# New hand-written orders for TensorE, ScalarE and VectorE in the first part of a fused attention and SwiGLU kernel

## The chip, the core and the metric

The kernel runs on one core of a Trainium2 chip. The metric is the device time of one execution in microseconds (us). In the profile PE is TensorE's matmuls, PEld its weight loads, DVE is VectorE, ACT is ScalarE, POOL is GpSimd and SP is SyncE. POOL and SP issue the transfers; POOL also does some masks, SP nothing else.

## The reference

Attention with 4 sink keys and a window of 128 keys, then a root-mean-square norm and a SwiGLU feed-forward layer (FFN):

```python
# q, k, v: (B, H, S, D) = (4, 8, 768, 64); n_sink = 4, window = 128
scores = q @ k.T / sqrt(D)
rel = pos[:, None] - pos[None, :]
keep = (pos[None, :] < n_sink) | ((rel >= 0) & (rel < window))
a = softmax(where(keep, scores, -1e9))
x = (a @ v).transpose(0, 2, 1, 3).reshape(3072, 512)
xn = x / sqrt(mean(x * x, -1) + 1e-6) * rms_g
g = xn @ w_gate                    # 512 x 1536
silu = g / (1 + exp(-g))
out = (silu * (xn @ w_val)) @ w_out   # w_out: 1536 x 512
```

Inputs and output are float32.

## The kernel before

**Tiling.** The 3072 tokens are 24 blocks g of 128 tokens, six per batch b. Four blocks make one of six FFN groups G of 512 tokens. A block is worked off in these steps; in the orders and below each has a short name:

- q, k and v of block g are loaded with a cast to bfloat16 (`load_bf16`, L353; `load_v`, L357) by POOL. The tile of v, `V16[b]`, holds the six blocks of a batch, with a 65th column per head that is 1.0, so that the product with v also gives the sum of the softmax. That column is written once per batch by a memset on DVE (L278, "vone:b"); the loads into this tile wait for it. The first load into each tile, in POOL's order, is v:0, v:8 (it stands ahead of v:6 and v:7), v:12 and v:18.
- q and k are transposed. Blocks 0 to 7: by PE (`pe_t`, L445) and a copy out of PSUM on DVE or ACT (`copy_t`, L452, "qT:g", "kT:g"). From block 8 on: by DMA transposes in SP's queue (`dma_t`, L459).
- Scores on PE (`scores` L485, `scores_last` L501, `tri_scores` L563, "s:g"). S:g needs k of block g and q of blocks g and g + 1. Scores of the sink keys are "ss" (L742).
- Exponentials on ACT ("x:g"), the mask on DVE (L520, L547, L584) or, from block 16 on, on POOL (L526, L597) ("e:g").
- The product with v on PE (`av`, L616, L621, L641), and the division by the sum on DVE (`normal`, L660, L661, "n:g").
- The square on ACT (`square`, L669, "ms:g"), and the norm on DVE (`rms`, L676 to L693, "xr:g").
- A transpose of the normalised block: by PE and a copy (L708, L714) up to block 7, by DMA in SP's queue (`dma_x`, L720) after that ("xt:g").

The FFN of a group runs over pieces (G, ft, column): gate matmuls (g, L975) and value matmuls (u, L975, out of `wv`), tanh on ACT (L982), `silu` (L988, "p1") and `hidden` (L998, "h", tile hT) on DVE, then the projections ("po", L1008), the copy to SBUF on ACT (L1016) and the store on SP (L1020). Group 0 is cut into pieces of 128 tokens and four column blocks of the weights (16 matmuls of 128 columns), groups 1 and 2 into pieces of 256 tokens and two column blocks (8 matmuls of 256 columns), the others into pieces of 512 tokens.

**The order.** No scheduler decides anything at build time. A class `Plan` numbers the operations as they are described (1077 of them). `ORDER` lists the numbers for each engine, `TURNS` says which engine's next operation is emitted at each step, and `BANKS` gives the PSUM bank of each tile of matmul results. `Plan.run` replays the three and asserts that each operation's needs have been given before. An engine works its list off in order. Each operation waits for what it reads and for the buffers that it writes; an operation that waits holds all that stand behind it on its engine, and a load that waits holds POOL's later loads and masks.

**The queues.** POOL's loads go in the order of `LOADS`, in which v:8 stands 33rd, behind the weights, and ahead of q:8, v:5, k:6, k:7, k:8, v:6, v:7 and q:9. The loads rotate through eight semaphores, so that a load is issued only when the load eight places ahead of it has landed. SP's queue begins with a few small loads; its transposes come in the order qT:8, qT:9, kT:8, kT:9, qT:10, qT:11, kT:10, kT:11, qT:12, qT:13, kT:12, kT:13, qT:14, then mixed with stores and xt.

In the description of the operations a few names only steer or check the plan: `LOAD_LEAD` and `T_LEAD` let a load or a transpose come only after a certain block's scores, `GATE_FROM` and `gate_of` tie the scores of a block to the progress of the FFN. They are requirements that `Plan.run` asserts, and issue no instruction.

Of the kernel before, what the change touches and what calls it, by code (L numbers as in the profile page):

```python
# [12 lines left out]
BF16 = mybir.dt.bfloat16  # L13
I32 = mybir.dt.int32

P = 128
# [18 lines left out]
class Plan:  # L35
# [33 lines left out]

ORDER = {  # L70
    "PE": """
# [18 lines left out]
""",  # L90
    "ACT": """
24 20 22 199 177 175 178 176 182 180 181 183 168 188 222 204-206 211 207 212 209 191 210
217 226 228 227 229 195 598 220 236 603 613 618 608 243 633 628 260 623 245 247 246 248
638 278 262 255 264-267 197 280 282 284 653 273 320 648 643 295 297 659 290 322 299 301
300 302 276 324 325 293 326 327 309 664 678 669 683 674 333 312 693 340 316 341 688 342
343 698 355-357 336 358 703 370 371 708 372 318 373 349 385 364 387 718 713 723 739 379
399 401 400 402 728 418 419 733 420 393 421 409 763 758 778 768 754 773 744 749 427 433
414 783 434-436 448 449 793 450 798 451 442 808 788 819 803 463-466 813 457 824 480 475
482 494 496 497 495 513 488 514 515 504 834 838 516 848 843 853 829 863 868 858 878 873
525 883 531-533 893 509 888 534 899 923 549-551 928 552 938 543 567-569 918 570 585 587  # L100
933 943 948 561 953 579 958 909 904 968 593 963 914 973 1008 1003 994 998 1013 1028 1023
989 1038 1018 1033 984 1053 1048 1043 979 1069 1059 1064 1072 1073
""",
    "DVE": """
# [24 lines left out]
""",  # L129
}  # L130
TURNS = """
ASDDSDGDPDPSPDPPPPPGPPPGPDPGPPDDPGAGPPPPADGPPPPGPPSPDPSADPGSDPSPGAAAPAGPAPPDAPPGPPAPDPAP
PPPADPGPDAGPPDPPDGAPPGPAPPAGDPAPAPDGADAPDGPAPPPADPAGPDAPADAGPPPPAPADGAPADGPPPPPAPPDPGPPD
DPAGPDPAGPDPGAPDDGPDGPDADGDPDGPADADPGAADPGPGDPADGAPDPGADAPGADADPGDPAPPDAPPDADAPGDPPADAGP
AAGPAPDAPPDPADPDAPGDAPDDGDPAPGDPPGSAAPGADAPGDPDGPPPDAGDAPGDADPPGADPAGDSAPPAGASPADPADSADP
PPGADAPGPSADDPGASAPGDPGSAPPGDPSADGAPDASDAPPDADPAGPPSAAADPAADPADPDAPAGADPGADPPDAPPADDPDGS
PDAPASAGDPPAPAGDSPADAPADDPPAGSADPPDASDPAGPADPSDDPGAPDDPADAPDGSDPDGPAGAPADSAPPADSDPPDGPDS
PDAGASPAAPDASGDPADSPDSDPGSPPPDDPSDGPDADPAPADPSDPSPDPSPDDAPDPDAPADPADAPDADAPDPDPASAPDASAP
DSADPADPDPASAPASADPAPPDASDPDAPSDASPADPDADPDPDPDAPASAPPDASADPAGPDGPGDPDGAPDPDPDPDAPAAGPSA
DGPAASGPADSPAGDPPGDDPGPPDGPDAAGPPDAGADPAGPAAGDPADAGPGPDSPGDPDASGPDGAADSPDAPDSDPPDSPDAPDS  # L140
ADPDSAPPDSDPSDAPDASPADDPDPDPADAPAAPDASADPADSPGSDGPDGSPGPGPAPAPADPAPDADPADAPDAGAPDGPGPAAP
AAPPADGDPPDGPDGDGPPAAPDSPGDPGAGPDAPPDPDPDPDAADPADPDDPAPAADPSDPDPDDPAAPPSPDDPAAPDPPSPPDPA
PSDSDSPASDPDPPPAAPDDPDPDPPAAPSDPDPAPDDPDPPPPAAPDADPSDPAAPDPDPAAPDDPDPDAPADPDPDPDPPDPAAPD
SPSDPPPPPAAPSASSPAADS
"""
BANKS = """
0123456701234567012345645645635654353513714370432704614654154761061305147237235720165760
7615743764051726351402376152376015237653746573746574631547613547647136210735462047136524
7012473650241762350741602735410721356421305406354063420675134632745013274350174362507431
6542371607152374153275461237104573604156324175032407615342047562310462317460170414217326  # L150
5047314243270172316412040572153042573045
"""


# [1 line left out]
def kernel(  # L156
# [15 lines left out]
    B, H, S, D = q.shape  # L172
# [29 lines left out]
    X_DMA_FROM = 8  # L202
    QK_DMA_FROM = 8
    LD = 16
    GATE_FROM = 8
    LOAD_LEAD = 10
    LEAD_FROM = 10
    WARM = 56
    GATE_LEAD = 14
    T_LEAD = 4  # L210
    SPLIT = (0,1)
    CHUNKS = (4,2,2)
    GB_PRIO = 2000
# [3 lines left out]
    HOST_FROM = 8  # L217

    const = ctx.enter_context(tc.tile_pool(name="const", bufs=1))
    ld = ctx.enter_context(tc.tile_pool(name="ld", bufs=LD))  # L220
    vld = ctx.enter_context(tc.tile_pool(name="vld", bufs=B))
    qkt = ctx.enter_context(tc.tile_pool(name="qkt", bufs=2))
    sink = ctx.enter_context(tc.tile_pool(name="sink", bufs=2))
# [108 lines left out]
        )  # L332

    for i in range(NS):
        sp(430, 2600, lambda i=i: load_sink(i), ["vsink1", "grow"], [("vsink", i)], -70 + i)

# [8 lines left out]
        eng.dma_start(out=T["st", name, g], in_=block_of(src, g))  # L345

    def cast(name, g, copy):
        T[name, g] = ld.tile([P, H, D], BF16, name=name)
        copy(out=T[name, g], in_=T.pop(("st", name, g)))

    def load_bf16(name, src, g):
        T[name, g] = ld.tile([P, H, D], BF16, name=name)
        nc.gpsimd.dma_start(out=T[name, g], in_=block_of(src, g))  # L353

    def load_v(g):
# [27 lines left out]

    def sw_block(g, what="qkv"):
        for n in what:
            needs = [("s", g - LOAD_LEAD)] if g >= LEAD_FROM else []
            if n == "v":
                sw_load(lambda g=g: load_v(g), [("v", g)], 860,
                        needs=needs + [("vone", g // NT)])
            else:  # L390
                src = q if n == "q" else k
                needs += [(n + "T", g - LD)] if g >= LD else []
                sw_load(lambda n=n, src=src, g=g: load_bf16(n, src, g), [(n, g)], 860,
                        needs=needs)
# [477 lines left out]
    for g in range(NB):  # L872
# [9 lines left out]
        for n in "qk":  # L882
            if g < QK_DMA_FROM:
                pe(225, lambda n=n, g=g: pe_t(n, g), [(n, g), "ident"] + old, [(n + "p", g)],
                   pa, takes=[(n, g)])
                ways = {"DVE": (345, lambda n=n, g=g: copy_t(n, g, nc.vector.tensor_copy)),
                        "ACT": (470, lambda n=n, g=g: copy_t(n, g, nc.scalar.copy))}
                either(ways, [(n + "p", g), "table"], [(n + "T", g)], early, drops=[(n, g)])
            else:
                sp(1290, 1200, lambda n=n, g=g: dma_t(n, g),  # L890
                   [(n, g)] + old + [("s", g - T_LEAD)], [(n + "T", g)], g,
                   ring="TR", work=1000)

        if t + 1 == NT:
# [57 lines left out]

        if t == 0:
            dve(600, lambda b=b: sink_k(b),
                [("kT", g), ("s", g + 1)] + ([("ss", b - 2, i) for i in ((2, 4) if b - 2 < 2 else (2,))]
                               if b >= 2 else []), [("ksk", b)], 0.1 * g)
            dve(640, lambda b=b: sink_v(b), [("vsink", i) for i in range(NS)] + ["headm"]
                + ([("av", NT * (b - 2) + NT - 1, u) for u in range(2)] if b >= 2 else []),
# [182 lines left out]
```

## Time and profile before

| | |
|---|---|
| median of 3 runs | 241.89 us (241.77 to 242.81) |
| profiled execution, span | 241.9 us |
| granted TensorE clock | 1.000 |
| DMA, software queue (POOL's loads) | 13.90 MB in 81760 packets, 79.3% of 16 engines' span |
| DMA, hardware queue q1 | 12.95 MB in 31810 packets, 29.8% |
| 0 to 22 us: PE busy, DVE busy | 18.75, 14.52 us |
| 22 to 72 us | 47.05, 44.34 us of 50 |
| 114 to 190 us | 75.15, 64.00 us of 76 |
| 190 to 241.9 us | 48.72, 24.69 us of 51.9 |

The span is the time from the first to the last instruction of one profiled execution. Busy time is the time in which the engine executed instructions; an engine with little idle time can't take more work without making the kernel longer. "L563" is a line of the code printed above. In a timeline each line has a start, a duration, the engine, the line and the operation with its tiles and shape; brackets hold the idle time of the engine just before it and what ended that. The "DMA to landing" of a load is the time from its issue to its completion.

### The profile page before, as it was taken

The numbers are of one execution on the slowest core, as the hardware profiler recorded it, in microseconds if no ns is written. First come the engines' busy times: TensorE is split into PE (matmuls) and PEld (weight loads), VectorE is DVE, ScalarE is ACT, GpSimd is POOL, SyncE is SP. The second block draws the span as 40 slices with busy tenths as digits, with TensorE's granted clock in tenths as the row PEclk, the third lists the DMA queues.
The fourth block names the chain that finished last, engine by engine and source line by source line (L and its number), as shares of the span: only waits on it lengthen the run. The fifth ranks groups of instructions, "written<-read, shape, count | busy, mean of one in ns | idle before, by whom it ended". The sixth has DMA issues, their size and how long they took to land.

```text
span 241.9 us, 5897 instructions
## 1 busy us (share of the span) xinstructions
PE 231.3 (96%) x2329; PEld 147.6 (61%) x2354; DVE 187.4 (77%) x478; ACT 122.8 (51%) x267; POOL 89.2 (37%) x116
## 2 busy tenths in 40 slices
PE   7889999999879999999999999999999999999995
PEld 5568986876668776777876644445554444444443
DVE  3599989989979999999898989994569946537520
ACT  4776368667766574337654464454543321233112
POOL 8985894597526554000004982022540000000000
PEclk9999999999999999999999999999999999999999
DMA  9999999999999999999601999527010114101024
GB/s 128 143 183 195 182 178 194 162 143 139 137 151 152 138 143 154 132 233 156 126 2 24 119 150 123 131 70 128 3 23 0 32 36 173 43 0 47 0 87 173
DMA packets 113741, 27.42 MB, mean 113 GB/s; under 512 B 103857, under 2 KB 110769, under 8 KB 113714
## 3 DMA queue, kind: packets, MB, share of 16 engines
q0 software_dynamic: 81760, 13.90, 79.3%
q1 hardware_dynamic: 31810, 12.95, 29.8%
q8 instruction: 18, 0.29, 0.5%
q10 hardware_dynamic: 144, 0.20, 0.2%
q14 instruction: 9, 0.07, 0.1%
HBM read 28.35 MB, written 6.29 MB: 143 GB/s over the span
## 4 chain that ended last, share of the span: by engine, by line
PE 67%; DMA 20%; POOL 6%; issue 2%; DVE 2%; SPq 2%; POOLq 0%
PE v L975 20%; PE o L1008 20%; PE g L975 18%; DMA wo<-in_moe_w_out_dram 5%; DMA qkT<-q 4%; DMA wv<-in_moe_w_val_dram 4%; DMA wg<-in_moe_w_gate_dram 3%; DMA q<-in_q_dram 3%; POOL v L357 2%; SPq L459 2%; PE s L563 2%; PE av L621 2%; POOL k L353 1%; PE av L616 1%; PE o_last L1028 1%
## 5 line engine op out<-in xcount | busy, mean ns | idle before, releaser
L975 PE MATMUL v<-xnt,wv 128*128 128x128 bf16 (+2 forms) x527 | 72.2, 282 | 0.4 <-DMA wv<-in_moe_w_val_dram 0.2
L975 PE MATMUL g<-xnt,wg 128*128 128x128 bf16 (+2 forms) x521 | 71.3, 281 | 0.4
L1008 PE MATMUL o<-wo,hT 128*128 128x512 bf16 x259 | 65.3, 379 | 1.1 <-issue 0.5
L982 ACT ACTIVATE th<-g 128x512 bf16<-128x512 f32 x72 | 41.7, 599 | 48.4 <-PE g L975 48.2
L988 DVE SCALAR_TENSOR_TENSOR p<-th,g 128x512 bf16<-128x512 bf16 x72 | 48.1, 682 | 18.9 <-ACT th L982 18.7
L975 PEld LDWEIGHTS <-wv 128*128 128x128 bf16 x528 | 43.3, 98 | 21.3 <-DMA wv<-in_moe_w_val_dram 0.6
L998 DVE TENSOR_TENSOR hT<-p,v 128x512 bf16<-128x512 bf16 x72 | 48.1, 682 | 9.3 <-PE v L975 7.8
L975 PEld LDWEIGHTS <-wg 128*128 128x128 bf16 x528 | 42.8, 98 | 19.3 <-issue 1.0
L1008 PEld LDWEIGHTS <-hT 128*128 128x128 bf16 x276 | 25.4, 98 | 26.5 <-issue 0.2
L597 POOL TENSOR_SCALAR_AFFINE_SELECT e<-e 128x512 bf16<-128x512 bf16 x20 | 12.7, 656 | 54.4 <-ACT e L572 53.0
L572 ACT ACTIVATE e<-s 128x384 bf16<-128x384 f32 x52 | 23.1, 495 | 12.5 <-PE s L563 12.5
L1016 ACT ACTIVATE osb<-o 128x512 f32<-128x512 f32 x23 | 13.4, 597 | 21.8 <-PE o L1008 18.0
L357 POOL DMA_DIRECT2D v<-in_v_dram x24 | 21.3, 888 | 8.5 <-DMA q<-in_q_dram 3.8
L353 POOL DMA_DIRECT2D q<-in_q_dram x23 | 20.4, 891 | 9.9 <-DMA k<-in_k_dram 6.7
L353 POOL DMA_DIRECT2D k<-in_k_dram x23 | 20.4, 889 | 9.1 <-DMA v<-in_v_dram 4.5
L669 ACT ACTIVATE sq<-x 128x512 bf16<-128x512 bf16 x24 | 15.1, 631 | 14.8 <-DVE x L661 14.5
L661 DVE TENSOR_TENSOR x<-av,rden 128x256 bf16<-128x256 f32 x48 | 20.4, 424 | 1.7
L693 DVE SCALAR_TENSOR_TENSOR xr<-x,r,gb 128x512 bf16<-128x512 bf16 x24 | 18.7, 778 | 0.8
L621 PE MATMUL av<-v,e 128*128 128x65 bf16 x192 | 16.4, 193 | 0.3 <-DMA v<-in_v_dram 0.3
L536 ACT ACTIVATE e<-s 128x512 bf16<-128x512 f32 (+1 forms) x36 | 15.1, 519 | 1.6 <-PE s L485 1.5
L616 PE MATMUL av<-v,e 128*128 128x65 bf16 x160 | 14.8, 193 | 0.0
L621 PEld LDWEIGHTS <-e 128*128 128x128 bf16 x192 | 12.7, 97 | 2.8 <-DVE e L547 0.4
(78 smaller groups left out, 192.6 us busy)
## 6 DMA issues: line engine op xcount, KB each, us to landing
out_dram<-osb SPq DMA_DIRECT2D x23, 256.0 KB, 2.2
v<-in_v_dram POOLq DMA_DIRECT2D x24, 128.0 KB, 8.9
q<-in_q_dram POOLq DMA_DIRECT2D x23, 128.0 KB, 8.1
k<-in_k_dram POOLq DMA_DIRECT2D x23, 128.0 KB, 9.6
wo<-in_moe_w_out_dram POOLq DMA_DIRECT2D x2, 768.0 KB, 11.3
wg<-in_moe_w_gate_dram POOLq DMA_DIRECT2D x5, 256.0 KB, 8.0
wv<-in_moe_w_val_dram POOLq DMA_DIRECT2D x5, 256.0 KB, 8.9
stage<-in_k_dram SPq DMA_DIRECT2D x1, 256.0 KB, 3.0
```

The lines of the kernel that those rows point to most:

```text
L353: nc.gpsimd.dma_start(out=T[name, g], in_=block_of(src, g))
L357: nc.gpsimd.dma_start(out=V16[b][:, t, :, 0:D], in_=block_of(v, g))
L572: nc.scalar.activation(out=e_tile(g)[:, x:x + 2, 0:TW], in_=BANK.pop(("s", g, u, hi))[:, 0:2 * TW].rearrange("p (j c) -> p j c", c=TW), fu ...
L616: nc.tensor.matmul(out=dest, lhsT=T["e", g - 1][:, x, P:2 * P], rhs=V16[b][:, t - 1, h, :], start=(t == 1), stop=False, skip_group_check=True,
L621: nc.tensor.matmul(out=dest, lhsT=T["e", g][:, x, 0:P], rhs=V16[b][:, t, h, :], start=(t == 0), stop=True, skip_group_check=True,)
L661: nc.vector.tensor_tensor(out=T["x16", g][:, 4 * u:4 * u + 4, :], in0=pvv[:, :, 0:D], in1=rden.unsqueeze(2).to_broadcast((P, 4, D)), op=AL ...
L693: nc.vector.scalar_tensor_tensor(out=T["xr", g], in0=T.pop(("x16", g)).rearrange("p h d -> p (h d)"), scalar=r[:, 3:4], in1=gb, op0=ALU.mu ...
L975: nc.tensor.matmul(out=ps[:, i * n:(i + 1) * n], lhsT=w_sb[:, kt, ft * P:(ft + 1) * P], rhs=T["xnt", G][:, kt, cols], start=(kt == 0), sto ...
L982: nc.scalar.activation(out=T["th", key], in_=BANK[("g", key)], func=ACT.Tanh, scale=0.5,)
L988: nc.vector.scalar_tensor_tensor(out=T["p1", key], in0=T.pop(("th", key)), scalar=1.0, in1=BANK.pop(("g", key)), op0=ALU.add, op1=ALU.mult,)
L998: nc.vector.tensor_tensor(out=T[hk][:, i:i + n, cols], in0=T.pop(("p1", key)).rearrange("p (n c) -> p n c", n=n), in1=BANK.pop(("v", key)) ...
L1008: nc.tensor.matmul(out=BANK[("o", G, tb)], lhsT=T["h", G, ft // 4][:, ft % 4, tb * P:(tb + 1) * P], rhs=wo[:, ft, :], start=(ft == 0), sto ...
```

## The change

The lists of PE, ACT and DVE in `ORDER`, and with them `TURNS` and `BANKS`, are replaced. The lists of POOL and SP are the same, and so are the operations. PE's list is the same again for its last 78 operations, ACT's for its last 37 and DVE's for its last 51. Six copies go from DVE to ACT (kT:0, qT:0, kT:1, kT:2, xt:2, xt:3), and four copies (qT:1, qT:2, qT:4, qT:6) and the cast of q:0 from ACT to DVE. The steering names that the new orders don't meet are dropped. The tiles of q and k keep sixteen buffers each, now as sixteen tags with one buffer. Lines behind L205 move up by five or less.

In DVE's list the memsets vone:1, vone:2 and vone:3 (operations 3, 4 and 5) stood 5th, 15th and 38th; now 3 stands between 256 (xr:3) and 635 (h) on one side and 268 (e:4) on the other, 4 between 344 (e:8) and 700 (h), 5 between 428 (xr:13) and 437 (e:14).

```diff
 ORDER = {
     "PE": """
-140 138 114 151 122 152 124 143 154 119 156 157 117 111 142 173 171 153 127 133 118 163
+161 117 162 134 127 137 143 138 139 131 150 166 129 114 121 149 113 112 130 148 173 171
...
-275 663 323 671 292 305 672 307 681 667 676 331 329 668 673 677 311 691 339 315 686 682
-696 354 687 697 335 347 345 692 701 369 706 317 360 362 707 702 384 736 375 716 711 737
-721 377 738 712 726 398 717 727 389 741 391 742 417 731 722 751 746 743 752 405 407 747
+642 292 652 323 671 305 307 686 672 673 676 329 681 331 687 682 311 677 696 691 339 315
+667 668 697 354 692 335 347 701 345 711 369 702 706 360 362 317 721 707 384 716 375
+736-738 377 712 717 726 731 398 732 741 727 722 389 751 391 417 746 405 752 742 407 743
...
     "DVE": """
-0 2 7 1 3 6 11 10 14 172 170 13 12 187 4 185 193 201 189 192 241 224 214 216 314 218 230
-231 233 235 599 237 600 239 604 605 614 5 619 615 620 609 634 610 629 624 625 630 249
-250 252 254 639 640 256 268 258 635 270 283 285 272 654 274 649 644 287 289 650 655 413
+7 0 1 14 2 6 11 10 22 199 13 193 12 185 187 222 189 216 241 214 192 218 231 230 599 235
+233 600 314 237 614 615 604 605 619 620 629 609 610 260 624 630 634 625 249 250 252 254
+295 639 256 635 3 268 640 283 270 272 285 649 274 654 650 287 289 644 291 313 645 303
+304 655 413 308 306 328 310 679 330 684 689 332 685 680 690 334 694 699 344 4 700 695
...
+770 779 780 784 774 775 785 428 5 437 794 441 452 795 789 439 799 790 809 443 800 456
...
@@
     LD = 16
-    GATE_FROM = 8
-    LOAD_LEAD = 10
-    LEAD_FROM = 10
+    GATE_FROM = NB
     WARM = 56
     GATE_LEAD = 14
-    T_LEAD = 4
@@
-    ld = ctx.enter_context(tc.tile_pool(name="ld", bufs=LD))
+    ld = ctx.enter_context(tc.tile_pool(name="ld", bufs=1))
@@
-        sp(430, 2600, lambda i=i: load_sink(i), ["vsink1", "grow"], [("vsink", i)], -70 + i)
+        sp(430, 2600, lambda i=i: load_sink(i), ["vsink1"], [("vsink", i)], -70 + i)
@@
-        T[name, g] = ld.tile([P, H, D], BF16, name=name)
+        T[name, g] = ld.tile([P, H, D], BF16, name=name, tag=f"{name}{g % LD}")
@@ def sw_block
-            needs = [("s", g - LOAD_LEAD)] if g >= LEAD_FROM else []
+            needs = []
@@
-                   [(n, g)] + old + [("s", g - T_LEAD)], [(n + "T", g)], g,
+                   [(n, g)] + old, [(n + "T", g)], g,
@@
-                [("kT", g), ("s", g + 1)] + ([("ss", b - 2, i) for i in ((2, 4) if b - 2 < 2 else (2,))]
+                [("kT", g)] + ([("ss", b - 2, i) for i in ((2, 4) if b - 2 < 2 else (2,))]
```

In PE's list 339 is s:8, 354 s:9, 369 s:10, 398 s:12 and 417 s:13; 681 and 682 are g and u of piece (1,2,0), 686 and 687 those of (1,4,0), 696 and 697 those of (1,8,0), 667 and 668 two projections of group 0, and 711 a gate of piece (1,2,256). In DVE's list 256 is xr:3, 344 e:8 and 428 xr:13.

More of the change, by code (lines that the diff above doesn't have):

```diff
@@ L91 @@
     "ACT": """
[L92 to L102, printed above, removed]
+24 20 172 170 177 175 180 178 176 201 182 168 181 188 183 206 204 207 211 209 205 212
+191 224 217 210 228 226 229 227 195 598 220 236 613 603 239 618 628 243 608 623 633 247
+245 248 246 638 278 262 255 197 264-267 280 258 282 648 284 273 653 643 320 297 290 659
+299 301 322 302 300 293 276 664 324-327 309 678 674 688 683 312 333 698 693 340-343 316
+669 355-357 336 358 703 370 371 713 372 349 318 373 385 708 387 718 364 739 723 728 733
+401 399 400 379 402 418-421 393 409 754 427 768 763 758 778 783 773 749 744 433 434 414
+435 436 448 449 793 450 451 788 798 819 808 442 463-466 813 803 457 480 482 496 497 494
[4 rows of a table added]
 """,
     "DVE": """
[10 rows of a table removed]
[10 rows of a table added]
 945 578 562 950 954 955 959 580 592 969 594 970 960 964 974 975 1009 965 1004 1010 999
@@ L131 @@
 TURNS = """
[L132 to L143, printed above, removed]
@@ L144 @@
-SPSDPPPPPAAPSASSPAADS
+ASDDDPSGPDPPDDPPSPPPPSPGPPGPDPGPSPPDPPPSGASGDPGPAPAPGPPDPPPDPGPPAPPAPPGPPPPAPDAAGADPPPPAGPPPAPPPPDAGPDGP
+PAPPDGAPPDPPGPPAPPPPAPPAPGAPAAGPDAPPADGDADGPAPADPAGAPAGPADAADGPDPPDGADPDAGDPADPGAPGDPGDPPDAGDPGAPADGAPDG
+PDAGDPGPDPGDAPADPADAPDAADPPDADPPDPAPDPADADPPADPAAPAPDAPPADDAGPPAGDPDGAPDAPGDPDAGDPDAGPSGPGDPDAGPPDAPGPDA
+DAGPADPGPAAGPAPADGPADPAGDASPDGAPADGSPADPPAGDSPADGDAPSPDSPAPAPADPADPDDPPADPDSADPADSDPAPAPSAPADPADAADPPASD
+DAPGPDAPAGDAPPAGDDPGDPAGAPADGADPAPSGDPPADAGSPDGPSGDPAAGPSAPAGDPASGDSPDGDPAPDADGPDPDDPGSADDPADPAGAPAPADSA
@@ new lines @@
+GDPSDPPDDSPDPPADSADPPDADPAAPPPDSPDSPSDPAPSPASDPSDPDSDAPAPPDSAADPDPSDPDADPDAPADADPADSPSDPADADPAAPAPDADGAP
+AGADPPGAPDDGPGPADDPADASPDDPASPADPADSPAAPSASDPGPDAGSDPGDGPDSAADPDPAPGAPGPASGPADGASDPGADPDGDPGPDDGPADAGPDG
+PPPGPADSADPPADPADAPAAGPADGAPDGPDAGDPGDPPDDAPAPAPDSPDPDASPDDSPDPDSDAPDASAPDADPSDPDSDPDPSASAPAADPSASDAPDAS
+PGDSGPADGDSPGDGPPAAPAPAPDADPAPDGDPGPAGAPAAPAPAPAAGPDGPDGDPGPDDPDPDPAAPPGDSPGDAGPDAPPDPDPDDPAADPADPDDPAPA
+APDSDPDPDPDAAPPPSDDPAADPPPSPPDPASPDSDSPASDPDPPPAADPDPDPDPPAASPDPDPADPDPDPPPPAADPADPSDPAAPDPDPAAPDDPDPDAP
@@ L145 @@
+APDDPDPDPPDPAADPSPSDPPPPPAASPASSPAADS
 """
 BANKS = """
[L147 to L151, printed above, removed]
+0123456701234567012345670123202102130130130134141241264260513531537153715715640731562743
@@ L152 @@
+0657342076435120635761243052436072436014305310435043512031540327514053724051432074321075
+6324163507216234065740176345201753462734027132476312342173206547312506731620735416207356
+1427327147526137012361705237654351425376014536025314025631476032517603471205715272371430
+6521472324315713470273525613764523614526
 """
@@ L347, in cast @@
     def cast(name, g, copy):
-        T[name, g] = ld.tile([P, H, D], BF16, name=name)
+        T[name, g] = ld.tile([P, H, D], BF16, name=name, tag=f"{name}{g % LD}")
         copy(out=T[name, g], in_=T.pop(("st", name, g)))
     def load_bf16(name, src, g):
-        T[name, g] = ld.tile([P, H, D], BF16, name=name)
+        T[name, g] = ld.tile([P, H, D], BF16, name=name, tag=f"{name}{g % LD}")
         nc.gpsimd.dma_start(out=T[name, g], in_=block_of(src, g))
```

36 rows, old and new, of the table ORDER are left out of this document.

## The prediction

> **What bounds the kernel now.** Read first are the page's busy times and slices: where PE is nearly full, only its gaps can be won.
>
> ```profile
> span 241.9 us, 5897 instructions
> ...
> PE 231.3 (96%) x2329; PEld 147.6 (61%) x2354; DVE 187.4 (77%) x478; ACT 122.8 (51%) x267; POOL 89.2 (37%) x116
> ...
> PE   7889999999879999999999999999999999999995
> ...
> DVE  3599989989979999999898989994569946537520
> ...
> PE 67%; DMA 20%; POOL 6%; issue 2%; DVE 2%; SPq 2%; POOLq 0%
> ```
>
> PE is idle for 241.9 - 231.3 = 10.6 us. A slice is 6.05 us; the only dent after the start is in the 11th and 12th slices (60 to 73 us). The last line is the chain that ended last: 67% PE, and 20% waits for transfers, all in the first part. Next is PE's timeline in that dent (start, duration, operation; in brackets the idle time before it and what ended it).
>
> ```profile
> 63.86 1.04 PE L975 MATMUL g<-xnt,wg 128*128 128x256 bf16 x8
> 65.68 0.54 PE L563 MATMUL s<-qkT 64*64 64x192 bf16 x24 [0.78 <-DMA qkT<-k]
> ...
> 68.13 1.04 PE L975 MATMUL g<-xnt,wg 128*128 128x256 bf16 x8
> 70.49 0.54 PE L563 MATMUL s<-qkT 64*64 64x192 bf16 x24 [1.32 <-DMA qkT<-q]
> ```
>
> These are the scores of blocks 8 and 9, the first whose q and k come through SyncE's DMA transposes. A gate group of eight 256-column matmuls takes 0.87 us from start to start (66.38 to 67.26, 67.26 to 68.13), so from 63.86 to 65.68 PE lost 1.82 - 0.87 = 0.95 us, and from 68.13 to 70.49 it lost 2.36 - 0.87 = 1.49 us: 2.44 together. The chain of waits says where the second wait comes from (start, duration, what):
>
> ```profile
> 47.27 7.30 DMA q<-in_q_dram
> ...
> 54.59 1.20 SPq L459
> ...
> 59.75 10.61 DMA qkT<-q
> ...
> 70.49 0.54 PE s L563 x16
> ```
>
> POOL's load of q 9 lands at 54.57; SyncE's queue, held there, goes on; qT:10 lands at 70.35. Last, a table of windows (core 0: length, then busy time of PE, PEld, DVE, ACT, POOL) for what follows, where DVE is nearly full too:
>
> ```profile
> 72.00:114.00 42.00, 41.68 (x465) 31.20 (x469) 39.80 (x107) 22.88 (x51) 13.11 (x15) 1.00 1.78 160
> ```
>
> **The change, part by part.** The sum is made against the profiled span, 241.88 us; the median of the runs shown is 241.89.
>
> *1. More FFN work ahead of the late scores.* No PE instruction is added or removed. Comparing the sets ahead of each score block, s:8 gets four groups more (g and u of (1,4,0), u(1,2,0), g(1,8,0)) and two projections fewer: net 2 x 0.87 = +1.75 us (a projection of four 512-column matmuls takes 0.86). Without its wait PE would reach s:8 at 63.86 + 0.87 = 64.73, with the change at 66.48, after kT:8's landing at 65.63: the 0.95 goes. S:9 also has +1.75 ahead (u(1,4,0), u(1,8,0), measured over the whole set): 70.49 - 2.44 + 1.75 = 69.80, while qT:10 lands at 70.35 and PE began 0.14 after that: 0.69 is left of the wait. Gain 2.44 - 0.69 = 1.75 us. What is late next: s:10 started at 75.38 and has +0.87 ahead, so 74.50, against kT:10 landed at 73.45 (1.05 to spare); s:12 87.50 + 1.75 - 1.75 = 87.50 against kT:12 at 84.21 (3.3 to spare); s:13 92.21 + 2.61 - 1.75 = 93.07 against qT:14 at 89.04 (4.0).
>
> *2. Three 98-ns memsets of V16's ones column go far back on DVE.* They ran by 27.6 us; now vone:1 stands behind xr:3, vone:2 behind mask e:8, vone:3 behind xr:13. Each is needed by a POOL load (v:8, v:12, v:18), and every later load stands behind it in POOL's queue.
>
> Vone:1: xr:3 ended at 41.32; one copy (0.41) comes ahead and one hT product replaces another: 41.7 + 0.1 = 41.8, so v:8 is issued at about 41.9 instead of 34.26. POOL's timeline:
>
> ```profile
> 34.26 0.87 POOL L357 DMA_DIRECT2D v<-in_v_dram  x1
> ...
> 39.20 0.88 POOL L353 DMA_DIRECT2D k<-in_k_dram  x1 [2.31 <-DMA wo<-in_moe_w_out_dram]
> ...
> 45.26 1.82 POOL L357 DMA_DIRECT2D v<-in_v_dram  x2 [2.60 <-DMA wo<-in_moe_w_out_dram]
> 47.27 0.87 POOL L353 DMA_DIRECT2D q<-in_q_dram  x1 [0.19 <-issue]
> ```
>
> And what one line's view says of v:5, v:6 and the last v:
>
> ```profile
> DMA to landing us min/median/max: 12.9/12.9/12.9
> ...
> DMA to landing us min/median/max: 7.0/7.0/7.0
> ...
> DMA to landing us min/median/max: 4.2/4.2/4.2
> ```
>
> V:5, issued at 35.99, took 12.9 us; v:6, issued 9.3 us later, 7.0; the last v, with little in flight, 4.2. V:8 landed at 46.99, v:5 at 48.86, v:6 at 52.26, q:9 at 54.57, evenly (0.7 to 1.3 us apart), though their issues have gaps of 2.3 and 2.6 us: in this stretch a load waits for those ahead of it, and a later issue shortens its wait, not its landing. The two wo loads and q:7 ahead end at 45.92, so v:8 at 41.9 has 5.1 us to its old landing and needs 4.2. At 0.9 us per issue q:9, eight loads on, goes out at 49.1 and has 5.5. Cost: 0 if loads drain in order; if each kept its latency, q:9's 1.8 us would pass through qT:9 and qT:10 to s:9, +1.8. I take 0, by the even landings; if the cover goes, each us of vone:1 beyond about 43 costs 1 us at s:9.
>
> Vone:2: e:8 ended at 70.76, and s:8 moves by 66.48 - 65.68 = +0.8, so 70 to 71.5. V:12 (58.11) is issued then, q:13 (59.41) 0.9 us later. The last load in flight, k:12, landed at 70.34: here the queue does run empty. At 4.2 us q:13 lands at about 76 instead of 74.78, at the 7.3 of q:9 at 79. SyncE waits for q:13 at qT:13, and kT:12, kT:13, qT:14 stand behind it: late by 1 to 4 us against 3.3 and 4.0 to spare. I take 0, as 4.2 is a row of a queue with few loads in flight, as this one would be; ends: 0, and 8.7 (15.4 us as q:13 had before: 71.4 + 15.4 = 86.8, 12.0 late, less 3.3).
>
> The Trainium skill, "DMA: Bandwidth & Descriptors", section on the anatomy of one DMA, gives 2.0 us plus bytes / 436e3 for such a load, an estimated 2.3 us for 128 KB; by it q:13 would land before 75 and the sum would be the same with more room. The row of 4.2 us is nearly twice that, and it is the row that is used.
>
> Vone:3: xr:13 ended at 113.17; v:18 goes from 87.36 to about 113, q:19 from a landing at 102.84 to about 118 (114 + 4.2), and holds SyncE's queue at qT:19 (111.26) until then: qT:18, xt:13, a store, kT:19, qT:20 follow. Next in SyncE's queue is xt:14, issued now only at 126.49, and s:18 began at 131.43: the work behind qT:19 took 118.44 + 1.2 - 111.26 = 8.4 us, so 126.4. Cost 0; at 7.3 us of landing, 3 us less room, up to +1.
>
> *3. Start and copies.* Twenty warm matmuls instead of 15 come ahead of the first mask; six copies go from DVE to ACT, four copies and the cast of q:0 the other way (about 0.4 us each). The first gate comes some 0.4 to 0.9 us later. PE waits for weights there (0.54 us lost at 30.31, for the wv load that lands at 30.08), which hides the first 0.5; the PE work ahead of s:3 (32.97) is the same but for one group in another's place. Cost 0 to 0.4; I take 0, as more than half lies under that load.
>
> *4. After the dent.* PE works ahead, but DVE has 42.00 - 39.80 = 2.20 us idle and must also get 1.75 ahead. Bounds 0 and +1.75. I take PE's loss of this stretch now once more, 42.00 - 41.68 = +0.32, since DVE has 50.00 - 44.34 = 5.7 us idle in 22 to 72 to draw on. PE's last 78 operations stand as before.
>
> Sum: 241.88 - 1.75 + 0.32 = 240.45, say 240.5 us.
>
> **Rivals.** *B, no change: DVE gives it back.* DVE, not PE, sets the pace from 72 to 114, and PE waits for e masks and normalisations. For it: 95% busy. Against: 2.20 us idle, more than 1.75. If the 1.75 goes back: 241.9 (241.2 to 242.6).
>
> *C, slower: the load queue runs empty at v:12 and restarts slowly.* Place: from vone:2 through q:13, SyncE's qT:13, kT:12 to s:12. Loss is q:13's latency beyond 71.4 to 78.1 us, that is beyond 6.7 us; at 8.1 the gain is gone, from 9.3 on it is slower by more than 1.21 us. At the 10.4 us that k:6 took, 81.8 is 7.0 late, less 3.3: +3.7, so 244.2; at 15.4, 249.2. For it: the median of all v loads is 8.9, and transposes load the same transfer engines. Against: the long latencies come with seven loads ahead, here there are none.
>
> The Trainium skill, "SBUF — State Buffer", section on two separate sides, says that a VectorE operation in a two-port mode keeps GpSimd from writing descriptors. Nine loads issued in a burst beside a full DVE would then be stretched; POOL's v loads took 873 to 974 ns each beside DVE at 95%, so the trace does not bear it out, and I give it no chance of its own.
>
> *D, a larger gain:* transposes land sooner with fewer loads beside them, and s:9's 0.69 goes too: 239.8, or 239.4 without the 0.32.
>
> *E, the change doesn't do what it says:* q:9 keeps its latency, so the wait moves back with the work: qT:10 1.8 later, s:9 at 72.29 with 1.75 more behind it, net +0.05, 241.9. Against it: the even landings of part 2.
>
> **How the numbers follow.** Forecast 0.45 (0.38 below 240.68, 0.07 above), B with E 0.20 (0.18 same, 0.02 slower), C 0.29 (0.27 slower, 0.02 same), D 0.06 (0.05 faster, 0.01 same). A measurement of this kernel tells 0.5%, 1.21 us, from no change. So faster 0.43, same 0.28, slower 0.29. The likeliest case's own range is 239.7 to 241.2. The range reaches down to D's 239.4, and up to 245.2, C at a latency of 11.4 us, leaving out the longer ones.
>
> **What would show it.** Right: no PE idle before s:8, under 0.8 us before s:9; v:8 issued near 42 and landed near 47, q:9 near 54.6; v:12 issued near 71 with q:13 landed before 78; s:12 started without a wait. Wrong: q:9 landed after 55.5 (part 2, vone:1); PE waiting for qkT at s:12 or s:13 (C); waits of PE for DVE between 72 and 114 above 1 us (B); s:3 later than 33.4 (part 3).

## The result: slower by 0.4 to 0.6%, with both forecast waits gone

After the change the kernel takes 242.85 us (median of 7 runs, 242.73 to 243.93) against 241.98 us for before beside it (7 runs, 241.47 to 242.81): ratio 1.0044, 95% interval 1.0024 to 1.0063. Run again beside its variants it took 243.30 against 241.91: 1.0062, 1.0043 to 1.0081. The forecast was 240.5.

The page of after, profiled in an execution of 243.44 us:

```profile
span 241.7 us, 5919 instructions
...
PE 234.2 (97%) x2354; PEld 149.1 (62%) x2354; DVE 187.6 (78%) x477; ACT 122.8 (51%) x268; POOL 90.8 (38%) x116
...
PE   8978999999999999999999999999999999999995
```

The dent in the 11th and 12th slices is gone. PE's timeline of after shows the scores of blocks 8 and 9 (L558 here) without any idle time in brackets:

```profile
65.56 1.91 PE L970 MATMUL g<-xnt,wg 128*128 128x256 bf16 x16
67.40 0.54 PE L558 MATMUL s<-qkT 64*64 64x192 bf16 x24
...
69.83 1.04 PE L970 MATMUL v<-xnt,wv 128*128 128x256 bf16 x8
70.80 0.54 PE L558 MATMUL s<-qkT 64*64 64x192 bf16 x24
```

The span is 241.7 and the time 243.44: 1.7 us lie around the span. All runs whose span is known, of all kernels, have 1.65 to 1.79 us there. So the span of 241.88 us from which the forecast started belongs to an execution of some 243.6 us (an estimate, 241.88 + 1.7), 1.7 us above before's median, and not to a median execution. This is where the explanation begins.

**Before, profiled again.** The same kernel, for the span of an ordinary execution.

> The kernel before, unchanged, to see how a run's time stands to its span. After's seven runs took 1.6 to 1.8 us more than their spans (242.73 against 241.0, 243.44 against 241.7). Theory 'outside': before has less time around its span, about 0 to 0.9 us (span near 241.5, time near 242.0), and the change lost 0.9 us outside the span. Rival 'slow profile': before has the same 1.7 us, its spans are near 240.3, and the profiled execution of 241.9 was a slow one, so that the change lost some 0.8 us inside the span.

It took 241.92 us (241.15 to 242.39), with spans of 239.4 to 240.7; the profiled execution has 240.3. The rival 'slow profile' holds. Its PE timeline:

```profile
65.50 0.54 PE L563 MATMUL s<-qkT 64*64 64x192 bf16 x24 [0.77 <-DMA qkT<-k]
...
68.92 0.54 PE L563 MATMUL s<-qkT 64*64 64x192 bf16 x24
```

S:8 waits as before, s:9 not at all: qT:10, issued at 59.57, landed at 68.0; in the execution shown at first it was issued at 59.75 and landed at 70.35. That is one transfer, landing 2.35 us apart in two executions of the same program. Of the 2.44 us of lost time from which the forecast started, this execution has 0.93. Three more profiles have before's lists up to there (the kernel with block 19's product earlier and two of the joined orders, all below): s:8 waits 1.09, 0.62 and 0.26 us in them, and s:9 never. So the wait at s:8 is usual and of changing size, and the wait at s:9 is rarer.

**Where the time went.** At a few places both orders have done the same PE work, so stretches between them can be compared (at the first, s:3, up to one FFN group in another's place). From PE's timelines, us from the first matmul of s:3 to the operation behind the first half of block 6's product (about 57 us), to the place behind block 8's product where both orders have done the same (74; in before s:10 comes next there), to s:15 (113), to the operation behind block 18's product (138), to s:21 (162), to the last projection but one:

```
                        s:3..57  ..74   ..s:15  ..138   ..s:21  ..end   sum
before, as shown          23.98  18.43   39.93   24.49   24.15  72.20  203.18
before, again             23.50  17.03   39.93   24.49   24.16  72.20  201.31
after                     23.74  16.46   40.02   25.05   24.88  72.19  202.34
after, again              23.73  16.46   40.02   25.05   24.87  72.20  202.33
after, memsets early      23.38  16.46   40.03   24.92   24.88  72.20  201.87
after, only vone:1 early  23.34  16.42   40.02   25.05   24.88  72.20  201.91
after, av:19 later        23.55  16.46   40.02   25.05   24.23  72.19  201.51
after, both               23.34  16.11   40.02   24.91   24.22  72.19  200.79
```

The last four rows are variants of after that the experiments explain; "both" has early memsets and block 19's product later. In the profiled execution of "both" the granted clock was 0.5 from 7.94 to 18.18 us and s:3 came some 4 us late, so only what stands behind s:3 is compared.

Against before again the change wins 0.57 us at blocks 8 and 9 and loses 0.24 ahead of them, 0.09 up to s:15, 0.56 from there to block 18's product and 0.72 around block 19: +1.04. Behind s:15 the stretches of one kernel repeat to 0.01 us; the second is the one that moves between executions of before's order: 17.03 and 18.43 here, and 17.40, 16.88 and 16.51 in the three other profiles just named. Without a wait it takes about 16.1 (16.11 in the last row). After's 16.46 is more than that: a gate group at 57.88 waits 0.21 us for an hT product of DVE, in which the rival 'DVE gives it back' shows.

The last two losses in PE's timeline of after:

```profile
137.06 0.54 PE L558 MATMUL s<-qkT 64*64 64x192 bf16 x24
...
138.92 1.02 PE L970 MATMUL g<-xnt,wg 128*128 128x512 bf16 x4 [0.23 <-DVE x L656]
...
145.41 0.20 PE L616 MATMUL av<-v,e 128*128 128x65 bf16 x1 [0.25 <-POOL e L592]
145.99 0.20 PE L616 MATMUL av<-v,e 128*128 128x65 bf16 x1 [0.34 <-POOL e L592]
```

and POOL's, for the masks of block 19 with a load between them:

```profile
141.68 2.17 POOL L592 TENSOR_SCALAR_AFFINE_SELECT e<-e 128x512 bf16<-128x512 bf16 x2 [3.55 <-ACT e L567]
143.80 0.90 POOL L348 DMA_DIRECT2D k<-in_k_dram  x1
144.70 1.23 POOL L592 TENSOR_SCALAR_AFFINE_SELECT e<-e 128x512 bf16<-128x512 bf16 x2
```

The new order comes to block 19's product at 144.97, 7.9 us behind s:19 (137.06); the masks end at 145.93. Before again has, on PE and on POOL:

```profile
136.75 0.54 PE L563 MATMUL s<-qkT 64*64 64x192 bf16 x24
...
147.95 0.19 PE L616 MATMUL av<-v,e 128*128 128x65 bf16 x1
...
143.48 1.44 POOL L597 TENSOR_SCALAR_AFFINE_SELECT e<-e 128x512 bf16<-128x512 bf16 x2
```

There the masks end at 144.92, but the product starts at 147.95, 11.2 us behind s:19: eleven gate and value groups stand between, not seven. The bracket at 138.92 is another matter: a gate waits for the PSUM bank that a normalisation on DVE (L656) has yet to empty, and DVE does the norm of block 16 (2 us, from 136.27) ahead of it:

```profile
137.57 0.75 DVE L688 SCALAR_TENSOR_TENSOR xr<-x,r,gb 128x512 bf16<-128x512 bf16 x1
138.24 0.18 DVE L655 RECIPROCAL rden<-av 128x4 f32<-128x4 f32 x1
138.45 0.42 DVE L656 TENSOR_TENSOR x<-av,rden 128x256 bf16<-128x256 f32 x1
```

### The profile page after: what moved, and what is told of

Its sections match the earlier page's. It is cut to its first block, busy times and chain, and to the rows that moved or that the text cites. A ratio compares the mean times of both kernels' runs of the same rounds, so it can differ in the third digit from the quotient of the medians.

```text
span 241.7 us, 5919 instructions
## 1 busy us (share of the span) xinstructions
PE 234.2 (97%) x2354; PEld 149.1 (62%) x2354; DVE 187.6 (78%) x477; ACT 122.8 (51%) x268; POOL 90.8 (38%) x116
## 4 chain that ended last, share of the span: by engine, by line
PE 75%; DVE 11%; DMA 4%; ACT 3%; issue 2%; POOL 2%; SPq 1%; POOLq 0%; DVEq 0%
PE g L970 23%; PE v L970 22%; PE o L1003 20%; DMA vsink<-in_v_dram 2%; DMA v<-in_v_dram 2%; PE s L558 2%; PE av L616 2%; DVE e L542 2%; DVE r L684 2%; DVE x L656 2%; DVE xr L688 2%; PE av L611 2%; ACT sq L664 1%; DVE hT L993 1%; PE o_last L1023 1%
## 5 line engine op out<-in xcount | busy, mean ns | idle before, releaser
L1003 PE MATMUL o<-wo,hT 128*128 128x512 bf16 x276 | 66.6, 379 | 0.0
L983 DVE SCALAR_TENSOR_TENSOR p<-th,g 128x512 bf16<-128x512 bf16 x72 | 47.7, 681 | 16.3 <-ACT th L977 16.1
L352 POOL DMA_DIRECT2D v<-in_v_dram x24 | 22.0, 917 | 48.5 <-DVE e L579 33.3
L567 ACT ACTIVATE e<-s 128x384 bf16<-128x384 f32 x52 | 22.6, 502 | 14.1 <-PE s L558 14.1
L592 POOL TENSOR_SCALAR_AFFINE_SELECT e<-e 128x512 bf16<-128x512 bf16 x20 | 13.7, 710 | 29.7 <-ACT e L567 29.5
L348 POOL DMA_DIRECT2D q<-in_q_dram x23 | 21.2, 923 | 2.3 <-PE s L480 1.0
L656 DVE TENSOR_TENSOR x<-av,rden 128x256 bf16<-128x256 f32 x48 | 20.4, 424 | 1.7
L348 POOL DMA_DIRECT2D k<-in_k_dram x23 | 21.1, 923 | 0.5 <-DMA wv<-in_moe_w_val_dram 0.4
L616 PE MATMUL av<-v,e 128*128 128x65 bf16 x192 | 17.0, 194 | 0.8 <-POOL e L592 0.6
L531 ACT ACTIVATE e<-s 128x512 bf16<-128x512 f32 (+1 forms) x36 | 15.6, 514 | 4.0 <-PE s L480 3.0
L611 PE MATMUL av<-v,e 128*128 128x65 bf16 x160 | 15.3, 193 | 0.0
```

Of the source, the lines that this page charges most:

```text
L352: nc.gpsimd.dma_start(out=V16[b][:, t, :, 0:D], in_=block_of(v, g))
L567: nc.scalar.activation(out=e_tile(g)[:, x:x + 2, 0:TW], in_=BANK.pop(("s", g, u, hi))[:, 0:2 * TW].rearrange("p (j c) -> p j c", c=TW), fu ...
L611: nc.tensor.matmul(out=dest, lhsT=T["e", g - 1][:, x, P:2 * P], rhs=V16[b][:, t - 1, h, :], start=(t == 1), stop=False, skip_group_check=True,
L616: nc.tensor.matmul(out=dest, lhsT=T["e", g][:, x, 0:P], rhs=V16[b][:, t, h, :], start=(t == 0), stop=True, skip_group_check=True,)
L656: nc.vector.tensor_tensor(out=T["x16", g][:, 4 * u:4 * u + 4, :], in0=pvv[:, :, 0:D], in1=rden.unsqueeze(2).to_broadcast((P, 4, D)), op=AL ...
L983: nc.vector.scalar_tensor_tensor(out=T["p1", key], in0=T.pop(("th", key)), scalar=1.0, in1=BANK.pop(("g", key)), op0=ALU.add, op1=ALU.mult,)
```

## The experiments

**After again**, beside variants of it.

> The kernel after the change, unchanged, beside its variants on one chip: 242.85 as before, span 241.1, with s:8 and s:9 free of waits and 0.9 us lost at the product of block 19.

It took 243.30 us (242.80 to 244.27). Its profiled execution (span 242.0) has the same stretches behind s:3, but s:3 at 34.00. DVE's timeline shows the first load of q late:

```profile
6.13 0.44 DVE L344 CAST q<-stage 128x512 bf16<-128x512 f32 x1 [2.90 <-DMA stage<-in_q_dram]
```

In the first profile of after that cast starts at 4.75, and s:3 at 33.65. Variants with the same start have s:3 at 33.0 to 33.3, as before does (32.97, 33.28), so the new order can start as early as the old one. Whether it starts late more often, these few profiles don't show.

**The late memsets.** The three moved to the front of DVE's list in after; then vone:1 alone; then, the other way, all three moved back in before. The diff shows the front of after's DVE list alone; further back in the list the three numbers are taken out.

```diff
-7 0 1 14 2 6 11 10 22 199
+7 0 1 14 2 3 4 5 6 11 10 22 199
```

> After with the three memsets of the ones column back at the start of DVE's list, nothing else. Theory 'held queue': in after PE lost 0.39 and 0.94 us at the products with v of blocks 18 and 19, whose POOL masks stand behind loads that vone:3 had held; with early memsets these go, 242.85 - 1.33 = 241.5. Against it a part: loads issued earlier run beside the transposes of blocks 8 to 10 again, and s:9's wait may come back by up to 0.7. Rival 'memsets are slack': 242.85 within 0.3, and the loss is elsewhere (the start: s:3 began at 33.65 instead of 32.97).

> After with only the first of the three late memsets (vone:1) back at the start of DVE's list; those ahead of v:12 and v:18 stay late. Theory 'only vone:1 costs' (v:5 and qT:8 land 0.2 to 0.9 later than in before, and PE waits at block 5's product and s:7): as after with all three early, 242.4, that is 0.45 below after. Rival 'vone:2 or vone:3 costs': 242.85 to 243.3, as after.

> Before with only the three memsets moved back on DVE to the places that they have in after (behind xr:3, mask e:8, xr:13), loads following in emission; PE, ACT and the rest of DVE as before. Theory 'held queue': 0.4 + 0.9 us lost at the products of blocks 18 and 19, but transposes land sooner while few loads are in flight (in after qT:10 landed at 68.31 against 70.35), so s:9's 1.49 shrinks by about 1 to 1.4: 242.0 + 1.3 - 1.2 = 242.1. Rival 'transposes don't care': 243.3. Rival 'the chain of waits is late by as much as the loads are issued later': q:9 plus 1 to 2 us, 243 to 245.

With all three early it took 242.38 us (242.11 to 244.11), 1.0017 of before (0.9994 to 1.0041). With vone:1 alone early it took 242.55 (242.38 to 243.13), 1.0028 (1.0011 to 1.0044). Both save 0.36 to 0.40 us of the first stretch of the table, so vone:1 is the one that costs there: 0.25 at block 5's product, where after's third matmul begins at 49.83 and v:5 has landed at 49.78, and 0.12 to 0.14 within s:7. Behind it all three early save another 0.13, at block 14's product; its cause stays open. The waits at blocks 18 and 19 stay in both: 'held queue' falls, they don't come from the loads that vone:3 had held.

In before the late memsets gave 242.39 (241.30 to 243.04), 1.0009 (0.9988 to 1.0029): no difference that can be told, against both rivals of 243 and more. The theory's time was 242.1, but not for its reason: blocks 18 and 19 take 24.49 and 24.16 us, as in before, so the loss that it counted on is not there. What it said of the transposes shows: in the profiled execution, the fastest of the twelve, qT:10 landed at 66.93, neither s:8 nor s:9 waits, and the second stretch takes 16.36 us. So in a profiled execution each of the two parts of the change is enough to take the forecast waits away, the late memsets in before's order and the new order with early memsets (16.46). Why the other executions of before with late memsets are not faster than before's stays open.

**Block 19's product.** In after its first half (operation 521) two FFN groups later; the same with the memsets early; and in before five groups earlier, which leaves six gate and value groups behind s:19, one fewer than after has.

```diff
 after, PE
-871 837 521 861 852 523
+871 837 861 852 521 523
 before, PE
-861 841 876 842 852 862 521
+861 521 841 876 842 852 862
```

> After with one change on PE: the first half of block 19's product with v goes two FFN groups later (behind the value group of piece (3,3,0)). Theory 'block 19 stands too near its scores': in after PE waits 0.94 us there for POOL's masks (it stands 8 us behind s:19, in before 11 us), and the wait goes: 242.85 - 0.95 = 241.9. Rival 'POOL's masks are the bound': the next half waits instead, and DVE and ACT follow later: within 0.3 of 242.85.

> After with early memsets and with the first half of block 19's product two FFN groups later. Theory: after with early memsets took 242.38; its wait of 0.95 at block 19 goes: 241.4. Rival 'the wait moves to the next half or to DVE': 242.2 to 242.6.

> Before with the first half of block 19's product five FFN groups earlier on PE (11.2 us behind s:19 became 6.9), as near as the change put it. POOL's masks of block 19 ended at 144.9 in before, the product would stand at 143.6. Theory 'block 19 stands too near its scores': PE waits 1.2 us: 241.95 + 1.2 = 243.1. Rival 'POOL would be earlier, or PE catches up': within 0.4 of 241.95.

The first took 243.15 us, but from 242.04 to 246.47, too wide to tell from after; in its profiled execution the stretch at block 19 falls from 24.88 to 24.23. With the memsets early it is clearer: 241.83 (241.41 to 245.71) against 242.38, and 0.9999 of before (0.9985 to 1.0013); the 241.4 expected was not reached. In before the edit costs far more than the 1.2 us expected: 249.48 (248.73 to 250.55), 1.0314 (1.0284 to 1.0344), with 32.22 us for the stretch instead of 24.16. PE's waits there:

```profile
144.28 0.20 PE L625 MATMUL av<-v,e 128*128 128x65 bf16 x1 [0.79 <-DMA k<-in_k_dram]
144.86 0.20 PE L625 MATMUL av<-v,e 128*128 128x65 bf16 x1 [0.35 <-POOL e L601]
147.46 1.87 PE L979 MATMUL g<-xnt,wg 128*128 128x512 bf16 x4 [1.41 <-DVE p L992]
155.27 1.04 PE L979 MATMUL v<-xnt,wv 128*128 128x512 bf16 x4 [2.53 <-DVE x L665]
```

The first two are the masks, and the load between them: 1.14 us, near the 1.2 expected. The others, 3.94 us, are DVE's: its list and ACT's were left as they were, and gates and value groups wait for PSUM banks that DVE empties in its old order. Together that is 5.1 of the 8.06 us by which the stretch is longer. Most of the rest is the clock of TensorE. In the wait ahead of 147.46 the granted clock fell to 0.5 and stayed there from 146.59 to 153.41 us; the third number from the end is the clock in that window:

```profile
146.60:153.40 6.80, 5.28 (x12) 1.62 (x11) 2.51 (x5) 1.55 (x4) 0.00 (x0) 0.50 0.53 99
```

The gate group at 147.46 took 1.87 us, where the one at 145.03 took 1.02, and the two value groups behind it 3.62 us: some 2.5 us more in all, an estimate from these rows. All six executions of this kernel have a mean clock below 1 (0.986 or 0.993). So this edit shows the wait for the masks, but its time is not the price of the nearness.

**Blocks 8 and 9.** In before the scores of block 8 one group later; then those of block 9 too.

```diff
-691 339 315 686 682 696 354 687 697
+691 686 339 315 682 696 354 687 697
 and
+691 686 339 315 682 696 687 354 697
```

> Before with one change on PE: the scores of block 8 (and the sink scores behind them) go one FFN group later, behind the gate group of piece (1,4,0). Theory 'the gain of the change is the wait at s:8': the wait of 0.93 us there shrinks to about 0.1, nothing else moves: 241.95 - 0.8 = 241.1. Rival 'the end is set elsewhere (DVE or the masks)': within 0.3 of 241.95.

> Before with the scores of block 8 one FFN group later (behind the gate group of piece (1,4,0)) and those of block 9 one group later too (behind the value group of the same piece). With block 8's alone later the time stayed at 241.78, and in its profiled execution PE waited 1.83 us at s:9: qT:10's landing sets s:9, whatever stands at s:8. Theory 'both must go': s:9 comes at about 68.9 as now, against qT:10 landed at 68.0 to 70.4, with one more group done: 0.87 gained in an execution where qT:10 lands at 68, up to 0.9 in others: 241.85 - 0.85 = 241.0. Rival 'DVE's masks of blocks 8 and 9 come later and hold the products behind them': within 0.3 of 241.85.

The first took 241.78 us (241.53 to 243.25), 1.0007 (0.9989 to 1.0024). Its profiled execution was its slowest, and there the wait stood at s:9:

```profile
65.87 0.54 PE L567 MATMUL s<-qkT 64*64 64x192 bf16 x24
70.16 0.54 PE L567 MATMUL s<-qkT 64*64 64x192 bf16 x24 [1.66 <-DMA qkT<-q]
```

The second is slower, at 242.71 us (242.19 to 243.59), 1.0034 (1.0021 to 1.0047). No transposed block is waited for any more, but

```profile
69.16 1.03 PE L979 MATMUL v<-xnt,wv 128*128 128x256 bf16 x8 [0.83 <-DVE hT L1002]
71.09 1.03 PE L979 MATMUL v<-xnt,wv 128*128 128x256 bf16 x8 [0.30 <-ACT e L576]
```

the value groups wait for DVE and ACT. These two edits of PE's list alone did not win the gain at blocks 8 and 9. That after has it because ACT's and DVE's lists were changed with PE's is likely, but not shown; moving three memsets in before's DVE list took the same waits away in the execution profiled above.

**One more repair.** After with early memsets and block 19's product later, and on DVE xr:16 (476) behind the normalisations of blocks 17 and 18.

```diff
 after, DVE
-485 476 501 487 503 489
+485 501 487 503 476 489
```

> After with early memsets, block 19's product two groups later, and on DVE the norm of block 16 (xr:16, 2 us) behind the normalisations of blocks 17 and 18, which hold PSUM banks that block 18's product and the gate of piece (3,2,0) wait for (0.39 and 0.25 us). Theory: 241.83 - 0.4 to 0.6 = 241.3, faster than before. Rival 'the wait moves on, to the transposes of block 16': 241.8 to 242.2.

It took 243.50 us (243.01 to 244.08), 1.0071 (1.0043 to 1.0098): slower. Block 18's waits go (its stretch is 24.52, as in before), and the next stretch grows to 26.03: PE waits 1.43 us at 144.95 for an hT product of DVE, and 0.26 at 149.31. So DVE's 2 us of norm, moved, hold PE at another place.

**Joined orders.** Six kernels take one kernel's lists up to a place and the other's behind it. At s:3 (before's first):

> The orders of before until the scores of block 3 are emitted, those of after from there on; the memsets are in the first part, so early. Theory 'start and held queue': the start's 0.7 us (s:3 back at 33.0) and the masks' 1.3 us go, the gain at s:8 and s:9 of 1.75 to 2.4 stays: 239.6 to 240.3. Rival 'the start costs nothing': the same as after with early memsets. Rival 'the gain goes back to DVE': 241.5 to 242.

At some 79 us:

> After's orders up to some 79 us (PE's first 180 operations; both kernels have done the same PE work there, so that the seam costs little), before's from there on; the three memsets at the start. Theory 'the gain is at s:8, the loss behind block 13': no wait at s:8, no waits at blocks 18 and 19: 241.95 - 0.9 = 241.0. Rival 'the first part is what costs': 242.4, as after with early memsets.

> The reverse: before's orders up to the same place, after's from there on, memsets early. Theory: s:8's wait stays (0.9), and blocks 18 and 19 cost 1.1 to 1.35: 241.95 + 1.2 = 243.1. Rival: 241.95 within 0.3.

At s:13, before's first, after's first, and after's first with early memsets:

> The orders of before until the scores of block 13 are emitted, those of after from there on. Theory 'the loss lies behind block 13': the waits at blocks 18 and 19 (0.4 and 0.95 us) come to the time of before, 241.97 + 1.35 = 243.3. Rival 'the loss lies in the first part' (start, late memsets): 242.0, as before.

> The orders of after until the scores of block 13 are emitted, those of before from there on; the first two late memsets are in it. Theory 'the loss lies behind block 13, the first part gains': s:8's 0.93 us gained, 0.4 lost at the product of block 5 and the scores of block 7 by the loads held for vone:1: 241.97 - 0.5 = 241.4. Rival 'the loss lies in the first part': 242.8.

> The same with the three memsets at the start of DVE's list. Theory 'late memsets cost 0.4': 241.0, faster than both kernels. Rival 'the hold of the loads lets the transposes land sooner, and early memsets give s:9's wait back': 241.4 to 242.

They took 243.71, 243.33, 244.27, 250.58, 252.27 and 251.73 us, all more than expected. As times they decide nothing: each has waits at or near its seam that neither kernel has (1.38 us behind s:3 in the first, 4.48 us ahead of a group at 106.20 in the fifth, behind which the granted clock is 0.5 for 6.83 us). Their stretches far behind the seam do say something: with after's lists there the stretches of blocks 18 and 19 take 24.88 to 24.92 and 24.87 to 24.88 us, with before's 24.49 and 24.15 to 24.16, whatever stands ahead. 'The loss lies behind block 13' holds for these two.

## Why the prediction was wrong, step by step

Two steps failed. Part 1 took a wait of 2.44 us as what every execution loses, and part 4 put all work behind the dent at +0.32 without comparing how far the products stand behind their scores. Against before again the terms measured -0.57 (part 1, forecast -1.75), +0.24 (ahead of the dent, forecast 0) and +1.37 (part 4, forecast +0.32): +1.04 in place of -1.43.

- *The sum's start.* "The median of the runs shown is 241.89" was set beside a span of 241.88 as if they were the same thing. The time holds 1.7 us more than the span; the profiled execution lay 1.7 us above the median, and 1.4 of this excess was the very wait that was to be won (18.43 against 17.03 in the table).
- *Part 1, the waits.* Right in mechanism: kT:8 and qT:10 landed at 66.26 and 68.31, and after reached s:8 at 67.40 and s:9 at 70.80. Wrong in size: 2.44 us were there in one execution, 0.93 in the other, and of five profiles with before's lists up to there only the first has a wait at s:9. Won at blocks 8 and 9: 18.43 - 16.46 = 1.97 against the first, more than the 1.75 forecast, and 17.03 - 16.46 = 0.57 against the second. That the first lies near the forecast is luck of the execution profiled.
- *Part 2, vone:1.* The memset ran at 42.49, v:8 was issued at 42.89 (41.9 forecast) and landed at 48.16 (47), q:9 at 55.40 (54.6). In-order draining held in the main: v:8, issued 8.6 us later than before, landed 1.2 us later and took 5.3 us, not 12.7. The cost was taken as 0; it is 0.36 to 0.40 us, inside the bounds of 0 and 1.8, and it is paid at block 5's product and at s:7, where the prediction did not look, and not at s:9.
- *Vone:2 and vone:3.* V:12 was issued at 72.82, q:13 at 73.68, landing after 4.1 us at 77.78; s:12 began at 87.80 without waiting for kT:12 (87.10), 0.7 us to spare. V:18 went out at 115.40. No wait for a transfer shows there, so the cost of 0 holds but for the 0.13 at block 14's product, which stays open. Rival C falls: the first loads after the pause took 3.7 and 4.1 us (v:12, q:13).
- *Part 3, the start.* S:3 at 33.65 and 34.00 would have passed the bound of 33.4, but kernels with the same start have 33.0 to 33.3, and the bound was passed by executions, not by the order alone. Why the first profile of after has 33.65, with q:0 on time, stays open.
- *Part 4, after the dent.* This is the other term that failed: +0.32 for all that follows. It measured 0.09 + 0.56 + 0.72 = 1.37; from 72 to 114, where the 0.32 was sought, it is 0.09. The prediction looked for late transfers and late scores and noted that PE's last 78 operations stand as before; it never compared, for the products, how far each stands behind its own scores. The distance for block 19 fell from eleven groups to seven, and the chain over ACT and POOL takes more than seven (8.9 us from s:19's start to the end of the masks in after, where the product came 7.9 us behind it). That this wait is the loss is shown: with the product two groups later the stretch takes 24.22 to 24.23 us in place of 24.88.
- *The rivals.* B has its result nearest (241.2 to 242.6) and the mechanism half: PE does wait for DVE, but at 57.88 and around block 18, not from 72 to 114, where after loses 0.09. D has the mechanism without the result: transposes did land sooner and s:9 does not wait. E falls: q:9 took 5.6 us, not 7.3.

With the two faults that experiments could take out, after is as fast as before and no faster by its times; its stretches add up to 200.79 against 201.31 us, which the times don't confirm, and that stays open. The rest, 0.42 us around block 18, goes when DVE's norm of block 16 is moved (24.52), and was not removed without a new loss.

## What to carry to other kernels

Before a forecast sells a wait, ask whether the execution profiled is an ordinary one: compare its time, not its span, with the other runs, and distrust a wait for a transfer in a single profile. When an order is rewritten, list for every consumer the work between it and its producer on the engine that sets the end, in both orders; a wait hidden before shows as a distance that has shrunk below the length of the chain between them. Changing one engine's list alone moved the wait to the engines that empty PSUM banks in three variants here. And where a variant has long waits, look at the granted clock before its time is read as the price of the edit.

## What was not expected of the hardware

With POOL's queue held, SyncE's transposes landed sooner. The transposes of q 12, issued at 68.16 in after, at 68.97 and at 67.56 in before's two executions:

```profile
DMA to landing us min/median/max: 4.8/4.8/4.8
```

```profile
DMA to landing us min/median/max: 7.7/7.7/7.7
```

```profile
DMA to landing us min/median/max: 8.5/8.5/8.5
```

These are the views of that line in after, before and before again. At that time after had one load in flight, k:12, and before had eight. The same shows in after again (4.7). Two variants show that it goes with the memsets and not with the new order. They are after with early memsets, with eight loads in flight (issued at 67.50), and before with late memsets, with one (issued at 68.12):

```profile
DMA to landing us min/median/max: 9.3/9.3/9.3
```

```profile
DMA to landing us min/median/max: 3.9/3.9/3.9
```
